# The down product of an MLP on taller tiles: 128 rows by 64 columns in a kernel of 64 by 64 tiles

## The chip, the cores and the metric

The kernel runs on one core of one Trainium2 chip, as a single program. The metric is the device time of one execution in microseconds; the number given for a kernel is the median of its runs. The core has a matrix engine (TensorE, PE in the profile, with its weight loads as PEld), a vector engine (VectorE, DVE), an activation engine (ScalarE, ACT), GpSimd (POOL), and the queue of SyncE (SP), which issues all DMAs of this kernel. Matmuls write into PSUM, which has banks of 512 float32 values in each of 128 partitions.

## The reference

An RWKV-7 recurrence over 768 steps, for 4 sequences and 8 heads of 40 channels, is followed by an MLP with the quick GELU. Everything is float32.

```python
# r, k, v, w, a, b: (4, 8, 768, 40); w_in: (320, 2048); w_out: (2048, 320)
for t in range(S):
    y[:, :, t] = einsum('bhd,bhde->bhe', r_t, state)
    Sa = einsum('bhde,bhe->bhd', state, a_t)
    state = state * w_t[:, :, None, :] - einsum('bhd,bhe->bhde', Sa, b_t) \
            + einsum('bhd,bhe->bhde', v_t, k_t)
x = y.transpose(0, 2, 1, 3).reshape(3072, 320)
h = x @ w_in
g = h * (1.0 / (1.0 + exp(-1.702 * h)))
return g @ w_out                      # (3072, 320)
```

The last line is what the change is about: 3072 tokens, a contraction over 2048, 320 columns out.

## The kernel before

**Units.** The recurrence is done in chunks of 64 steps. A unit is one chunk of two sequences, so there are 24 units (`NU`), two for each of the 12 chunks. For every unit the kernel builds decay factors (`decay`), scaled operands and score matrices (`prep`, PSUM tiles `ps_A` and `ps_RV`), inverts a triangular matrix by repeated products (`inverse`, `ps_N`, five steps `ps_level`, `ps_Q`, `ps_T`), and solves and advances the state (`solve`: `ps_zT`, `ps_rz`, `ps_B`, `ps_X`, `ps_y`). The result goes through DRAM (`x_dram`) and comes back turned as `xT_all`.

**The MLP.** As soon as both units of a chunk are there, `mlp(c)` works on its 256 tokens. `up` computes 128 hidden channels for 256 tokens at a time, `gelu` (L1023) writes them to `g` as float32 with the channels on the partitions: a tile of `g` holds two channel groups `m` of 2 x 128 channels. `down(p)`, for `p` in 0 and 1, contracts them with `w_out_sb`, whose rows are the same channels, into 128 tokens by 320 columns. Its eight parts `part(m)`, for `m` in 0 to 7 (`NM`), each take two groups `f` of 128 channels, and all add into the same pair of PSUM banks.

**Tiles of the array.** Every matmul in the kernel works on a tile of at most 64 rows by 64 columns, and works are laid out in fours, in the order of `QUARTERS`: the row half `r` of the operands and the column half `b` of the output. In the down product the two row halves of a group of 128 channels are contracted in different quarters and land in different banks, `po[HALF[b], r]`. So bank 0 holds the sum over the channels in partitions 0 to 63 and bank 1 that over partitions 64 to 127, and L1047 copies the first to `ob` (on ACT or DVE, whichever is free by the plan) while L1049 adds the second (on DVE). Then `store` (L1046) issues two DMAs to `out`. A float32 product is two MATMUL instructions and two LDWEIGHTS; all are recorded at line 332, the helper `mm`, so the profile is read by tiles: `ps_down` is the down product, `ps_up` the up product. 12 chunks x 2 halves x 8 parts x 2 groups x 4 quarters x 2 instructions are the 3072 matmuls of `ps_down`.

**The order.** Nothing is issued as it is written. Each piece of work is handed to `plan.add` with a rank, a time on each engine that may do it, what it reads and writes, and the PSUM pair that it uses; there are four pairs of banks. `Plan.order` is a simulation in the host program: each engine that comes free takes the task of the lowest rank that is ready. Attention tasks have low ranks and MLP tasks 10000 and up, so the MLP fills the time in which no attention task is ready. PE's tasks also carry `instr`, a number of instructions: the plan believes that PE's instructions are fetched in blocks of 256 (`fetched`, `ahead`), and passes over a task whose instructions would come too late. `paced` spreads the MLP over the time, and `refined` tries 300 random changes to the ranks of the opening's tasks and keeps those that shorten the plan. The order that results is fixed: the engines then run it with semaphores.

The price of a PE task comes from one line:

```python
return {"PE": sum(n * 2 * max(m[0] / 1.2 + 5 if m else 58.0, cols / 1.2 + 3) for n, cols, *m in sets),
        "instr": sum(16 * n for n, *_ in sets)}
```

Of the kernel before, what the change touches and what calls it, by code (L numbers as in the profile page):

```python
# [279 lines left out]
def rwkv7_gelu_quick(ctx: ExitStack, tc: tile.TileContext, time_d, v_d, w_d, wc_d, ak_d, b_d, rv_d, w_in, w_out, out):  # L280
    nc = tc.nc
    H, D, S = 8, 40, out.shape[0] // 4
    DM = H * D
# [7 lines left out]
    NQ = NM // 2  # L291
# [9 lines left out]
    HALF = [slice(0, 64), slice(64, 128)]  # L301
    CHANNELS = [slice(h.start, h.start + D) for h in HALF]
    BITS = (0, 1)
    QUARTERS = [(0, 0), (1, 1), (0, 1), (1, 0)]
# [7 lines left out]
    plan = Plan(dict(logw=3, wc=3, G=1, wch=3, wz=2, time=2, ak=2, b=2, rv=2, FT=3, GT=1, kh=2, bh=2, zr=2, rz=2,  # L312
                     A=1, B=1, RV=2, E0=2, W0=2, P21=2, PT=2, W=2, E=2, ES=2, EX=2, T=2, Tc=1, QT=1, zraw=2, zT=1, M=2, x=1, xT=3, g=4, ob=1), 4)
# [5 lines left out]
    def buf(name, n, shape, dt=FP32):  # L319

        if (name, n) not in tiles:
            s = n % plan.slots[name]
            tiles[name, n] = work.tile(shape, dt, tag=f"{name}{s}", name=name)
        return tiles[name, n]

    def psum(t, name):
        if t.pair not in psums:
            psums[t.pair] = banks.tile([128, 2, 512], FP32, tag=f"pair{t.bank}", name=name)
        return psums[t.pair]

    def mm(o, lhsT, rhs, start):
        nc.tensor.matmul(o, lhsT, rhs, start=start, stop=True, skip_group_check=True)  # L332
# [5 lines left out]
    def pe(*sets):  # L338

        return {"PE": sum(n * 2 * max(m[0] / 1.2 + 5 if m else 58.0, cols / 1.2 + 3) for n, cols, *m in sets), "instr": sum(16 * n for n, *_ in sets)}  # L340

    def dve(n):
        return {"DVE": 170.0 + 1.03 * n}
# [4 lines left out]
    def any2(n):  # L348
        return {**act(n), **dve(n)}

    def copy(e):
        return nc.scalar.copy if e == "ACT" else nc.vector.tensor_copy
# [99 lines left out]
    w_out_sb = w_sb[:, NK * NM * 128:]  # L452
# [555 lines left out]
    ob_of = lambda n: buf("ob", n, [128, DM])  # L1008

    def mlp(c):  # L1010
        R = 10000 + 100 * c

        def up(q, m, k):
            def go(t):
                ph, x = psum(t, "ps_up"), xT_of(c)[:, :, k]
                for r, h in QUARTERS:
                    mm(ph[HALF[h], r, m * 256:(m + 1) * 256], w_in_sb[HALF[r], 2 * q + m, k, h * 64:(h + 1) * 64], x[HALF[r]],
                       m == 0 and k == 0)
            plan.add(R + q, pe((1, 256)), go, reads=[("xs", (c, p)) for p in BITS] + [("weight", q)],
                     uses=[("xT", c)], room=[("g", c * NQ + q)], pair=("up", c * NQ + q), most=1)  # L1020

        def gelu(q):
            plan.add(-45, {"ACT": 1030.0, "table": "gelu"}, lambda t: nc.scalar.activation(  # L1023
                g_of(c * NQ + q).rearrange("p m r n -> p r m n"), psum(t, "").rearrange("p r (m n) -> p r m n", m=2),
                ACT.Gelu_apprx_sigmoid), writes=[("g", c * NQ + q)], pair=("up", c * NQ + q))

        def down(p):
            serial = 2 * c + p

            def part(m):  # L1030
                def go(t):
                    po, g = psum(t, "ps_down"), g_of(c * NQ + m // 2)[:, m % 2]
                    for f in (2 * m, 2 * m + 1):
                        for r, b in QUARTERS:
                            o = p * 128 + b * 64
                            mm(po[HALF[b], r, :DM], g[HALF[r], f % 2, o:o + 64], w_out_sb[HALF[r], f * DM:(f + 1) * DM], f == 0)
                parts = range(2 * m * DM // PIECE, (2 * (m + 1) * DM - 1) // PIECE + 1)
                plan.add(R + 10 * (p + 1) + m, pe((2, 320)), go, reads=[("g", c * NQ + m // 2)] + [("weight", NQ + n) for n in parts],
                         pair=("down", serial), most=1)
            for m in range(NM):  # L1040
                part(m)

            def store(t):
                for b in BITS:
                    o = (2 * p + b) * S + c * C
                    nc.sync.dma_start(out[o:o + C, :], ob_of(serial)[HALF[b]])  # L1046
            plan.add(-45, any2(320), lambda t: copy(t.engine)(ob_of(serial), psum(t, "")[:, 0, :DM]),  # L1047
                     writes=[("ob", serial)], pair=("down", serial))
            plan.add(-45, dve(320), lambda t: nc.vector.tensor_add(ob_of(serial), ob_of(serial), psum(t, "")[:, 1, :DM]),  # L1049
                     reads=[("ob", serial)], writes=[("out", serial)], pair=("down", serial))  # L1050
            plan.add(-100, {"SP": 700.0}, store, reads=[("ob", serial), ("out", serial)], size=128 * DM * 4)

        for q in range(NQ):
            for m in BITS:
                for k in range(NK):
                    up(q, m, k)
            gelu(q)
        for p in BITS:
            down(p)
# [110 lines left out]
```

## Time and profile before

| | |
|---|---|
| median of 3 runs | 695.43 us |
| the runs | 690.06, 695.43, 698.79 us |
| span of the profiled execution | 691.5 us, 42207 instructions |
| its own time | not given apart from the span; the median of the runs stands 3.9 us above the span |
| busy: PE / weight loads / DVE / ACT / POOL | 655.2 / 532.6 / 437.5 / 363.7 / 204.4 us |
| `ps_up` matmuls | 3840, 251.1 us busy, mean 377 ns |
| `ps_down` matmuls | 3072, 238.8 us busy, mean 430 ns |
| `ps_down` weight loads | 3072, 124.8 us busy, mean 133 ns |
| the adds of L1049 | 24, 11.6 us busy, mean 483 ns |
| mean granted TensorE clock | 0.987 |

The busy time of a group is the time in which at least one of its instructions runs, so matmuls that run side by side count once; the mean is that of one instruction. The page cuts the span in 40 slices and gives each engine's busy share in tenths. The chain that ended last follows the work back from the last instruction, at each step to what released it. A number in brackets behind an instruction in a timeline is the engine's idle time before it, and who ended it.

### The profile page before, as it was taken

The page shows a single profiled execution, that of the slowest core. Times are in us where ns is not written, and L with a number is a line of the kernel's source. Part 1 is how long each engine was busy: PE and PEld are TensorE (multiplying, and loading weights), DVE is VectorE, ACT ScalarE, POOL GpSimd, SP SyncE. Part 2 cuts the span into 40 slices and gives each one's busy share as a digit, 9 for nine tenths or more (in the row PEclk, how much of TensorE's full clock was granted, in tenths as well). Part 3 has the DMA queues.
Part 4 walks back from the last instruction along what each step waited for, and adds up shares of the span by engine and source line. Part 5 has one row for each costly group of instructions (what it writes and reads, how often), then busy time and mean ns, then how long its engine had stood idle before and what let it go on. Part 6 is the DMA issues. An engine that isn't in the chain of part 4 may idle for free.

```text
span 691.5 us, 42207 instructions
## 1 busy us (share of the span) xinstructions
PE 655.2 (95%) x19488; PEld 532.6 (77%) x19488; DVE 437.5 (63%) x799; ACT 363.7 (53%) x760; POOL 204.4 (30%) x258
## 2 busy tenths in 40 slices
PE   5676899999999999999999999999999999999997
PEld 4575777878899889878798787787779777786663
DVE  7777888657767667857676856776776656542000
ACT  4566565565555664564645566547555544432020
POOL 6546563232133242343132424222222331100000
PEclk9979999999999999999999999999999999999999
DMA  7985443233322531441331432331431320111000
GB/s 257 344 276 178 143 151 97 80 104 87 98 79 70 135 121 33 120 126 54 110 103 58 124 100 82 109 100 48 136 116 43 108 68 17 42 42 32 21 3 20
DMA packets 35312, 69.73 MB, mean 101 GB/s; under 512 B 5440, under 2 KB 14656, under 8 KB 35136
## 3 DMA queue, kind: packets, MB, share of 16 engines
q1 hardware_dynamic: 35136, 67.03, 32.0%
q8 instruction: 153, 2.51, 1.5%
q14 instruction: 23, 0.19, 0.1%
HBM read 59.15 MB, written 7.86 MB: 97 GB/s over the span
## 4 chain that ended last, share of the span: by engine, by line
PE 88%; DMA 4%; DVE 3%; issue 2%; ACT 2%; SPq 0%; ACTq 0%; DVEq 0%
PE ps_up L332 29%; PE ps_down L332 28%; PE ps_level L332 8%; PE ps_y L332 5%; PE ps_B L332 5%; PE ps_X L332 3%; PE ps_N L332 2%; PE ps_rz L332 1%; DMA time<-in_time 1%; PE ps_RV L332 1%; PE ps_A L332 1%; PE ps_zT L332 1%; DMA w_sb<-in_w_in 1%; PE ps_Q L332 1%; PE ps_cum L332 1%
## 5 line engine op out<-in xcount | busy, mean ns | idle before, releaser
L332 PE MATMUL ps_up<-xT_all,w_sb 64*64 64x256 f32 x3840 | 251.1, 377 | 0.8 <-DVE E L788 0.5
L332 PE MATMUL ps_down<-w_sb,g 64*64 64x320 f32 x3072 | 238.8, 430 | 1.2 <-DVE ob L1049 1.1
L332 PEld LDWEIGHTS ps_up<-xT_all,w_sb 64*64 64x64 f32 x3840 | 153.0, 133 | 30.1 <-issue 1.7
L332 PEld LDWEIGHTS ps_down<-w_sb,g 64*64 64x64 f32 x3072 | 124.8, 133 | 49.9 <-PE ps_RV L332 0.7
L1023 ACT ACTIVATE g<-ps_up 128x1024 f32<-128x1024 f32 x48 | 49.2, 1025 | 34.1 <-PE ps_up L332 33.4
L662 POOL TENSOR_TENSOR kh<-time,G 128x320 f32<-128x320 f32 x24 | 21.8, 906 | 143.2 <-PE ps_y L332 56.9
L332 PEld LDWEIGHTS ps_level<-W,EX 64*64 64x64 f32 x2560 | 56.9, 134 | 8.4 <-issue 0.9
L786 ACT COPY W<-ps_level 128x512 f32<-128x512 f32 x49 | 28.7, 586 | 65.4 <-PE ps_level L332 65.3
L742 ACT ACTIVATE EX<-ES,quads 128x256 f32<-128x256 f32 x92 | 41.7, 501 | 39.1 <-DVE ES L737 39.1
L332 PE MATMUL ps_level<-W,EX 64*64 64x64 f32 (+1 forms) x2560 | 55.5, 218 | 0.0
L788 DVE TENSOR_TENSOR E<-two,ps_level 128x256 f32<-128x256 f32 x80 | 33.2, 415 | 26.3 <-ACT W L786 25.6
L1049 DVE TENSOR_TENSOR ob<-ob,ps_down 128x320 f32<-128x320 f32 x24 | 11.6, 483 | 59.4 <-ACT ob L1047 59.1
L332 PE MATMUL ps_level<-PT,EX 64*64 64x64 f32 (+2 forms) x1280 | 33.9, 238 | 10.7 <-DVE EX L758 5.9
L332 PEld LDWEIGHTS ps_level<-PT,EX 64*64 64x64 f32 x1280 | 31.2, 141 | 16.0 <-issue 4.3
L654 POOL TENSOR_TENSOR ak<-ak,FT 128x512 f32<-128x512 f32 x20 | 27.9, 1394 | 50.8 <-DMA ak<-in_ak 22.7
L926 ACT COPY B<-ps_B 128x416 f32<-128x416 f32 (+1 forms) x39 | 19.1, 491 | 43.2 <-PE ps_B L332 43.2
L737 DVE STREAM_TRANSPOSE ES<-E 128x256 f32<-128x256 f32 x80 | 35.6, 445 | 4.2
L988 POOL TENSOR_TENSOR x<-zr,FT 128x128 f32<-128x128 f32 x72 | 36.1, 530 | 1.8 <-DVE zr L978 1.8
L832 ACT COPY Tc<-ps_level 32x64 f32<-32x64 f32 x134 | 27.1, 202 | 18.1 <-PE ps_level L332 15.9
L732 POOL TENSOR_TENSOR PT<-two,PT 128x256 f32<-128x256 f32 x20 | 14.6, 730 | 72.4 <-DVE PT L724 72.4
L332 PE MATMUL ps_y<-M,bh 64*64 64x104 f32 (+1 forms) x768 | 34.6, 246 | 0.1
L332 PE MATMUL ps_y<-RV,kh 64*64 64x104 f32 (+1 forms) x768 | 34.4, 247 | 0.0
(134 smaller groups left out, 1157.2 us busy)
## 6 DMA issues: line engine op xcount, KB each, us to landing
time<-in_time SPq DMA_DIRECT2D x24, 320.0 KB
ak<-in_ak SPq DMA_DIRECT2D x48, 160.0 KB
rv<-in_rv SPq DMA_DIRECT2D x48, 160.0 KB
xT_all<-x_dram SPq DMA_DIRECT2D x48, 160.0 KB
wc<-in_wc SPq DMA_DIRECT2D x20, 264.0 KB
logw<-in_w SPq DMA_DIRECT2D x24, 160.0 KB
RV<-in_v SPq DMA_DIRECT2D x24, 160.0 KB
b<-in_b SPq DMA_DIRECT2D x48, 80.0 KB
```

What stands on the lines that cost most here:

```text
L332: nc.tensor.matmul(o, lhsT, rhs, start=start, stop=True, skip_group_check=True)
L654: plan.add(R, {"DVE": 690.0, "POOL": 1270.0, "sbuf": True}, lambda t: of(t.engine).tensor_mul(ahT(), ahT(), FT_of(i)), reads=T("ak", "FT") ...
L662: plan.add(R + 4, {"POOL": 870.0, "DVE": 490.0, "sbuf": True}, lambda t, n=n, dst=dst: of(t.engine).tensor_mul(dst(i)[:, :, :D], by_head(t ...
L732: plan.add(R, {"DVE": 430.0, "POOL": 750.0, "sbuf": True}, lambda t: of(t.engine).tensor_sub(at(W0_t, i)[:, :, :32], two32.unsqueeze(1).to ...
L737: plan.add(rank, dve(256), lambda t: nc.vector.transpose(ES(n), source(t)), writes=[key("ES", n, 6)], **reads)
L742: nc.scalar.activation(dst[:, :, h], ES(n), ACT.Copy, scale=quads[:, h, :1])
L786: plan.add(rank, any2(512), lambda t: copy(t.engine)(tiles_of(W(n + 1)), blocks(psum(t, ""), 64)), writes=[key("W", n + 1, 5)], pair=pair)
L788: plan.add(rank, dve(256), lambda t: nc.vector.tensor_sub(tiles_of(E(n + 1)), every(two32, [128, 2, 4, 32]), blocks(psum(t, ""), 64)[:, :, ...
L832: copy(t.engine)(dst, src[:, u, :, f])
L926: plan.add(R, any2(4 * wide), lambda t: copy(t.engine)(dst(), some(psum(t, "")[:, :, :208])), writes=[("Bv", i)] if x and c > 0 else T("B" ...
L988: of(t.engine).tensor_mul(x[:, b ^ u, b], both(i)[:, at, :64], FT_of(i)[:, at])
L1023: plan.add(-45, {"ACT": 1030.0, "table": "gelu"}, lambda t: nc.scalar.activation(g_of(c * NQ + q).rearrange("p m r n -> p r m n"), psum(t, ...
```

## The change

The quarters of the down product become halves: for each group of 128 channels there are two matmuls, one for each column half `b`, with all 128 partitions of `g` as weights (64 tokens, the columns of the tile) and all 128 partitions of `w_out_sb` as the moving operand. Both write to bank 0 of the pair, to partitions 0 to 63 and 64 to 127. The sum over the row halves is made in the contraction, so the second bank stays unused, L1049 goes, and the store waits for the copy of L1047 alone. The plan keeps the old price of a part on PE, and its number of instructions is set from 32 to 16. All other products keep tiles of 64 by 64.

```diff
                     for f in (2 * m, 2 * m + 1):
-                        for r, b in QUARTERS:
+                        for b in BITS:
                             o = p * 128 + b * 64
-                            mm(po[HALF[b], r, :DM], g[HALF[r], f % 2, o:o + 64], w_out_sb[HALF[r], f * DM:(f + 1) * DM], f == 0)
+                            mm(po[HALF[b], 0, :DM], g[:, f % 2, o:o + 64], w_out_sb[:, f * DM:(f + 1) * DM], f == 0)
                 parts = range(2 * m * DM // PIECE, (2 * (m + 1) * DM - 1) // PIECE + 1)
-                plan.add(R + 10 * (p + 1) + m, pe((2, 320)), go, ...
+                plan.add(R + 10 * (p + 1) + m, {**pe((2, 320)), "instr": 16}, go, ...
...
             plan.add(-45, any2(320), lambda t: copy(t.engine)(ob_of(serial), psum(t, "")[:, 0, :DM]),
                      writes=[("ob", serial)], pair=("down", serial))
-            plan.add(-45, dve(320), lambda t: nc.vector.tensor_add(ob_of(serial), ob_of(serial), psum(t, "")[:, 1, :DM]),
-                     reads=[("ob", serial)], writes=[("out", serial)], pair=("down", serial))
-            plan.add(-100, {"SP": 700.0}, store, reads=[("ob", serial), ("out", serial)], size=128 * DM * 4)
+            plan.add(-100, {"SP": 700.0}, store, reads=[("ob", serial)], size=128 * DM * 4)
```

More of the change, by code (lines that the diff above doesn't have):

```diff
@@ L1033, in go @@
                     for f in (2 * m, 2 * m + 1):
-                        for r, b in QUARTERS:
+                        for b in BITS:
                             o = p * 128 + b * 64
-                            mm(po[HALF[b], r, :DM], g[HALF[r], f % 2, o:o + 64], w_out_sb[HALF[r], f * DM:(f + 1) * DM], f == 0)
+                            mm(po[HALF[b], 0, :DM], g[:, f % 2, o:o + 64], w_out_sb[:, f * DM:(f + 1) * DM], f == 0)
                 parts = range(2 * m * DM // PIECE, (2 * (m + 1) * DM - 1) // PIECE + 1)
-                plan.add(R + 10 * (p + 1) + m, pe((2, 320)), go, reads=[("g", c * NQ + m // 2)] + [("weight", NQ + n) for n in parts],
+                plan.add(R + 10 * (p + 1) + m, {**pe((2, 320)), "instr": 16}, go, reads=[("g", c * NQ + m // 2)] + [("weight", NQ + n) for n in parts],
                          pair=("down", serial), most=1)
```

## The prediction

> **What bounds the kernel now.** I read the page first: busy shares, the slices, then the chain that ended last.
>
> ```profile
> PE 655.2 (95%) x19488; PEld 532.6 (77%) x19488; DVE 437.5 (63%) x799; ACT 363.7 (53%) x760; POOL 204.4 (30%) x258
> PE   5676899999999999999999999999999999999997
> ...
> PEclk9979999999999999999999999999999999999999
> ...
> PE 88%; DMA 4%; DVE 3%; issue 2%; ACT 2%; SPq 0%; ACTq 0%; DVEq 0%
> PE ps_up L332 29%; PE ps_down L332 28%; PE ps_level L332 8%; PE ps_y L332 5%; PE ps_B L332 5%; PE ps_X L332 3%; PE ps_N L332 2%; PE ps_rz L332 1%; DMA time<-in_time 1%; PE ps_RV L332 1%; PE ps_A L332 1%; PE ps_zT L332 1%; DMA w_sb<-in_w_in 1%; PE ps_Q L332 1%; PE ps_cum L332 1%
> ...
> L332 PE MATMUL ps_down<-w_sb,g 64*64 64x320 f32 x3072 | 238.8, 430 | 1.2 <-DVE ob L1049 1.1
> ```
>
> TensorE sets the end: 88% of the chain, of which the down product 28%, at full granted clock after the opening. A busy PE need not be a full one, so the second view is the chain in order of time, to see how fast the stream runs; first its last stretch of matmuls, then a piece from the middle.
>
> ```profile
> 671.61 15.12 PE ps_down L332 x224
> ```
>
> ```profile
> 333.77 1.08 PE ps_down L332 x16
> 334.85 0.71 PE ps_B L332 x32
> 335.57 1.08 PE ps_down L332 x16
> 336.64 0.71 PE ps_B L332 x32
> 337.36 1.08 PE ps_down L332 x16
> 338.43 0.46 PE ps_level L332 x32
> ```
>
> 224 matmuls are 56 sets of four quarters, so a set takes 15.12/56 = 0.270 us, although one matmul lasts 430 ns: four quarters stream side by side and the next set starts 160 ns before the last is through. All of the product is 3072/4 = 768 sets, 207 us. In the middle piece a part (16 matmuls, 4 sets) takes 1.08 us, the same rate: there is no slack in it. The piece shows too that single parts of the down product are laid between tasks of the attention. Counted over the whole timeline (fragments of one to three instructions at the seams put to their neighbours), the product stands in 140 stretches, most of one part. The last stretch ends the stream, so there are 140 entries and 139 exits: 279 seams.
>
> The third view, PE's timeline, shows what happens at a seam (start, length, then the work).
>
> ```profile
> 337.15 1.29 PE L332 MATMUL ps_down<-w_sb,g 64*64 64x320 f32 x16
> 338.22 0.67 PE L332 MATMUL ps_level<-W,EX 64*64 64x64 f32 x32
> 338.69 1.29 PE L332 MATMUL ps_down<-w_sb,g 64*64 64x320 f32 x16
> ```
>
> The next task starts 337.15 + 1.29 - 338.22 = 0.22 us before the down matmuls are through, and the next down part 0.20 us before the level is. That overlap is what the whole schedule lives on, and the change touches it.
>
> **Part 1: the streaming.** Removed are 1536 matmuls and 1536 weight loads (f: two tiles for four quarters). A set becomes two tiles of 128 rows by 64 columns, each streaming the same 320 columns. The column halves already run side by side now, and the rows of one tile work at once, so a set stays at 0.270 us and the product at 207 us: cost 0. If the two tiles ran one after the other it would cost 768 x 0.270 = 207 us; that is a rival below. The work does not shrink, because half as many instructions use twice the rows each.
>
> **Part 2: the weight loads.** A load is hidden now: in the view of loads one part's 16 loads run in 0.74 us beside matmuls that take 1.31.
>
> ```profile
> 115.30 0.74 PEld L332 LDWEIGHTS ps_down<-w_sb,g 64*64 64x64 f32 x16
> ```
>
> All 16 are done while the four sets still stream, so a quarter is loaded ahead while its own matmul runs. I take the same for the taller tile: 0. Cover gone, a load holds its tile back by what a matmul of a cold start is longer: this tile's matmuls last 429 ns in the median and at most 480, so 51 ns; per set 51 (both tiles at once) to 102 ns (in turn), 768 sets: 39 to 78 us.
>
> ```profile
> L332 PEld LDWEIGHTS ps_down<-w_sb,g x3072: 129/133/140, 89.8 to 686.0; 64*64 64x64 f32 x192
> L332 PE MATMUL ps_down<-w_sb,g x3072: 426/429/480, 90.0 to 686.3; 64*64 64x320 f32 x192
> ```
>
> The Trainium skill speaks against me here: "TensorE: Matmul & The Clock Gate", Part 3, says that a weight load overlaps running matmuls only where the row group differs. Two tiles of 128 rows always share all row groups, so by this rule no load would hide. The row above contradicts it for the quarters; no run here shows it for 128 rows.
>
> **Part 3: the seams.** All matmuls of the kernel now work on tiles of at most 64 by 64; the only other shapes are parts of such a tile (40 rows, 40 columns). After the change each of the 279 seams is a change from a tile that lies over two row halves to one that lies over one, or back. The trace has no such change, so I bound it. From below: at the seam of down and the 40-row read (in the timeline a stretch of two parts starts at 330.92, plus 2 x 1.08 gives 333.08, and the read starts at 333.10) nothing is lost: 0 ns, 0 us in all. From above: no overlap at all and a whole weight load, 0.22 + 0.133 = 0.35 us, 279 times: 98 us. Between them I take a restart in which the old matmuls must be out of the array before the new tile's weights can go in: the 429 - 270 = 159 ns that a matmul stays behind its stream, plus the 51 ns of an uncovered load: 0.21 us, 279 x 0.21 = 59 us. I choose it and not 0 because one contraction over both row halves needs both at once, so a quarter that is not yet through must hold it up, where the 40-row piece lies in a quarter of its own; the nearest row is then a matmul that starts with nothing loaded ahead. Behind each wait everything on PE is queued, and PE is the bound; ACT's gelu (L1023), DVE's masks and the attention's copies wait for PE and slip with it.
>
> The Trainium skill states that changing the tiling mode drains TensorE ("TensorEngine Tiling (Array Packing)", Key Properties); it gives no time. With it the term cannot be 0; without it the bounds above stand.
>
> **Part 4: the second bank and the add.** 24 tensor_add (L1049) of 486 ns go: 11.6 us of DVE, which has 63% load and is not on the chain, hidden behind PE's stream, 0. If that cover were gone they would have cost 11.6. On the path they stand in two places. At the end:
>
> ```profile
> 686.75 0.43 ACT L1047 COPY ob<-ps_down 128x320 f32<-128x320 f32 x1 [8.19 <-PE ps_down L332]
> 687.21 0.49 DVE L1049 TENSOR_TENSOR ob<-ob,ps_down 128x320 f32<-128x320 f32 x1 [8.12 <-ACT ob L1047]
> 687.73 1.11 SPq L1046 DMA_DIRECT2D out<-ob  x2
> ```
>
> The store is issued about 0.5 us sooner: -0.5. And PE with its loads waited 1.1 + 0.5 = 1.6 us on this add before it could reuse the pair of banks; now it waits for the copy, 0.5 us earlier: take half, -0.8. The store's two issues on SP stay as they are; they only lose a wait.
>
> **Part 5: the planner.** It prices a part as before (2 x 2 x (320/1.2 + 3) = 1079 ns, the 1.08 of the chain) but counts 16 instructions for 32, so its rule on PE's instruction fetch bites less and the order will differ. PE's stream shrinks from 38,976 matmuls and loads by 3072 (8%). From 100 us on, the waits put down to "issue" before PE and its loads add up to some 10 us, so the gain lies between 0 and 10; I take 2, since few of these waits stand at the down product (0.7 before its loads).
>
> The other order may move the opening, where PE idles 19 + 8 = 27 us of the first 100; I set 0 with 5 either way, an estimate of a fifth of that.
>
> **Sum.** 691.5 (span) + 59 - 0.5 - 0.8 - 2 = 747. The page gives a span alone for the profiled execution; the median of the runs, 695.4, stands 3.9 above it, which I add: 751, rounded to **750 us**.
>
> **Rivals.**
>
> Not slower: seams are free (0 ns as at the 40-row seam). Then only part 4 and 5 remain: 695.4 - 1.3 - 0 to 10, so 684 to 694, likeliest 691. For it: no seam in the trace costs anything. Against it: no seam in the trace joins tiles of different heights. It decides when a seam costs less than 1.3 + 2 over 279, about 12 ns. Chance 0.18.
>
> Taller loads are not hidden: 750 + 39 to 78 = 789 to 828. For: no 128-row load in the trace. Against: quarters are loaded under their own matmul. Chance 0.10.
>
> The column tiles run one after the other, so the change does not do what its unchanged price in the plan says: 750 + 207 = 957. Against: column halves already overlap in every set of 0.270 us. Chance 0.06.
>
> The forecast's own case, seams between 51 ns (a load alone, 14 us) and 0.30 us (84 us): chance 0.66, range 706 to 776.
>
> **Range and chances.** From 694 to 800: left out are the gaining part of the first rival (0.11), the upper part of the second (0.03) and the third (0.06). Two per cent, about what a measurement of this kernel tells from no change, is 14 us: faster needs below 681.5, which takes the first rival's whole gain and a luckier opening, 0.05; the same takes the rest of the first rival and seams of barely a load, 0.17; slower the rest, 0.78.
>
> **What will show it.** Right: the down product's part still near 1.08 us inside a stretch of several parts, PE's time between two stretches grown by about 0.2 us at each seam, in the timeline no overlap between down and its neighbours, the last long stretch of 224 (then 112) matmuls still near 15.1 us, a lower share of busy PE. Wrong: seams that overlap by 0.2 us as now (first rival), or a last stretch of 20 us or more (second) or 30 (third). Far fewer stretches than 140 would make my count wrong, not the price.

## The result: 5% slower, and the profile after

The changed kernel takes 729.5 us (median of 4 runs, 728.3 to 730.1) against 694.1 us for the kernel before (4 runs, 690.1 to 698.8). The ratio is 1.050, with a 95% interval of 1.045 to 1.055: 35 us more. The profiled execution has a span of 728.4 us and its own time is 730.1.

From the page of the changed kernel, the lines that answer to those of before:

```profile
PE 693.5 (95%) x17952; PEld 485.9 (67%) x17952; DVE 419.8 (58%) x780; ACT 348.9 (48%) x728; POOL 220.6 (30%) x276
PE   5567999999999999999999999999999999999997
...
PE 87%; DMA 7%; DVE 2%; issue 1%; SPq 1%; POOL 1%; ACT 0%; DVEq 0%; POOLq 0%; ACTq 0%
...
L332 PE MATMUL ps_down<-w_sb,g 128*64 128x320 f32 x1536 | 237.2, 441 | 0.0
```

PE has 1536 matmuls fewer and 38 us more of busy time, and its share is the same 95%. So PE's share does not show where the time went: a matmul's end is modelled, and PE counts as busy through the pauses shown below. The share of the weight loads fell from 77% to 67%, but half as many loads for the down product lower it by themselves: a kernel below that has their old number again is as slow and has 81%. What gives the time away is why the loads were idle. Their row in the page before, then after:

```profile
L332 PEld LDWEIGHTS ps_down<-w_sb,g 64*64 64x64 f32 x3072 | 124.8, 133 | 49.9 <-PE ps_RV L332 0.7
L332 PEld LDWEIGHTS ps_down<-w_sb,g 128*64 128x64 f32 x1536 | 97.9, 136 | 81.6 <-issue 10.8
```

"issue" is time in which an engine waited for nothing that the profile shows. Over all weight loads the waits put to it add up to 19 us before and 68 us after.

The chain in order of time (start, length up to the next piece, work) tells more. First the last stretch of the down product, then a piece from the middle.

```profile
708.87 15.25 PE ps_down L332 x112
```

```profile
344.46 1.23 PE ps_down L332 x8
345.69 1.59 PE ps_B L332 x64
347.28 1.23 PE ps_down L332 x8
348.50 0.62 PE ps_A L332 x32
```

112 matmuls are 56 sets of two tiles in 15.25 us, 0.272 us per set: the taller tile streams at the old rate, side by side, with its loads hidden. But a part between two attention tasks takes 1.23 us instead of 1.08, and the task before a part is longer as well: 64 matmuls of `ps_B` take 1.59, where two pieces of 32 took 0.71 each. So each seam costs some 0.15 to 0.17 us here. The product stands in 138 stretches, so there are 275 seams.

PE's timeline at such a seam (start, length as modelled, work):

```profile
343.85 0.62 PE L332 MATMUL ps_level<-W,EX 64*64 64x32 f32 x32
344.39 1.30 PE L332 MATMUL ps_down<-w_sb,g 128*64 128x320 f32 x8
345.62 0.59 PE L332 MATMUL ps_B<-RV,A 64*64 64x104 f32 x16
```

Of the overlap of 0.22 and 0.20 us before, 343.85 + 0.62 - 344.39 = 0.08 and 0.07 are left. And the tile's view gives the longest matmul, 484 - 432 = 52 ns above the median. Exactly the first two matmuls of each of the 138 stretches are this long: their weights were not loaded ahead.

```profile
L332 PE MATMUL ps_down<-w_sb,g x1536: 432/432/484, 96.0 to 723.7; 128*64 128x320 f32 x192
```

The end of the program, as foreseen, is shorter without the add: from the start of the last copy to the store it is 0.45 us instead of 0.98.

```profile
724.19 0.43 ACT L1047 COPY ob<-ps_down 128x320 f32<-128x320 f32 x1 [8.19 <-PE ps_down L332]
724.64 1.11 SPq L1046 DMA_DIRECT2D out<-ob  x2
```

### The profile page after: what moved, and what is told of

Read it like the earlier page. It is cut to its first block, busy times and chain, and to the rows that moved or that the text cites. A ratio compares the mean times of both kernels' runs of the same rounds, so it can differ in the third digit from the quotient of the medians.

```text
span 728.4 us, 39081 instructions
## 1 busy us (share of the span) xinstructions
PE 693.5 (95%) x17952; PEld 485.9 (67%) x17952; DVE 419.8 (58%) x780; ACT 348.9 (48%) x728; POOL 220.6 (30%) x276
## 4 chain that ended last, share of the span: by engine, by line
PE 87%; DMA 7%; DVE 2%; issue 1%; SPq 1%; POOL 1%; ACT 0%; DVEq 0%; POOLq 0%; ACTq 0%
PE ps_down L332 31%; PE ps_up L332 28%; PE ps_level L332 7%; PE ps_y L332 4%; PE ps_B L332 4%; PE ps_X L332 2%; DMA rv<-in_rv 2%; PE ps_N L332 1%; PE ps_rz L332 1%; PE ps_A L332 1%; PE ps_RV L332 1%; DMA wc<-in_wc 1%; PE ps_zT L332 1%; PE ps_T L332 1%; DMA x_dram<-x 1%
## 5 line engine op out<-in xcount | busy, mean ns | idle before, releaser
L332 PE MATMUL ps_up<-xT_all,w_sb 64*64 64x256 f32 x3840 | 245.5, 379 | 1.1 <-issue 0.5
L332 PE MATMUL ps_down<-w_sb,g 128*64 128x320 f32 x1536 | 237.2, 441 | 0.0
L332 PEld LDWEIGHTS ps_up<-xT_all,w_sb 64*64 64x64 f32 x3840 | 140.5, 134 | 44.7 <-issue 7.7
L332 PEld LDWEIGHTS ps_down<-w_sb,g 128*64 128x64 f32 x1536 | 97.9, 136 | 81.6 <-issue 10.8
L786 ACT COPY W<-ps_level 128x512 f32<-128x512 f32 x57 | 33.4, 586 | 72.6 <-PE ps_level L332 72.5
L742 ACT ACTIVATE EX<-ES,quads 128x256 f32<-128x256 f32 x98 | 44.5, 501 | 37.3 <-DVE ES L737 36.8
L332 PEld LDWEIGHTS ps_level<-W,EX 64*64 64x64 f32 x2560 | 50.2, 134 | 17.8 <-issue 9.5
L988 POOL TENSOR_TENSOR x<-zr,FT 128x128 f32<-128x128 f32 x80 | 41.1, 543 | 3.2 <-issue 2.7
L744 POOL TENSOR_TENSOR EX<-ES,quads 128x512 f32<-128x512 f32 x15 | 20.3, 1351 | 49.4 <-DVE ES L737 47.2
L744 POOL TENSOR_TENSOR T<-ES,quads 128x512 f32<-128x512 f32 x12 | 15.9, 1323 | 58.2 <-DVE ES L737 58.2
```

The costliest lines, as they stand in the source:

```text
L742: nc.scalar.activation(dst[:, :, h], ES(n), ACT.Copy, scale=quads[:, h, :1])
L744: of(t.engine).tensor_mul(dst, ES(n).unsqueeze(2).to_broadcast([128, 8, 2, 32]), quads.unsqueeze(1).to_broadcast([128, 8, 2, 32]))
L786: plan.add(rank, any2(512), lambda t: copy(t.engine)(tiles_of(W(n + 1)), blocks(psum(t, ""), 64)), writes=[key("W", n + 1, 5)], pair=pair)
L988: of(t.engine).tensor_mul(x[:, b ^ u, b], both(i)[:, at, :64], FT_of(i)[:, at])
```

## The experiments

Theory S says that each seam between tile shapes costs about 0.155 us. The rivals are O, that the other order and the other instruction count cost the time, and P, that each set of the taller tile costs more wherever it stands.

**Tile and order apart.** The first kernel has the new tiles in the old order, the second the old tiles in the new order. The second leaves out the sum of the second bank, so its output is not the whole product.

```diff
 e1: the kernel before, with
-  for r, b in QUARTERS: mm(po[HALF[b], r, :DM], g[HALF[r], ...], w_out_sb[HALF[r], ...])
+  for b in BITS:        mm(po[HALF[b], 0, :DM], g[:, ...], w_out_sb[:, ...])
-  lambda t: nc.vector.tensor_add(ob_of(serial), ...)
+  lambda t: None
 e2: the changed kernel, with
-  for b in BITS:        mm(po[HALF[b], 0, :DM], g[:, ...], w_out_sb[:, ...])
+  for r, b in QUARTERS: mm(po[HALF[b], r, :DM], g[HALF[r], ...], w_out_sb[HALF[r], ...])
```

> Taller tiles, but in the order of the kernel before: the plan gets the old number of instructions and the old task of the add, which issues nothing. 140 stretches of the down product, so 279 seams. Theory S (each seam between tiles of 64 by 64 and of 128 by 64 costs about 0.155 us, from the changed kernel's trace: a part takes 1.23 us up to the next task instead of 1.08, and the task before a part 0.16 us longer): 694 + 279 x 0.155 = 737 us, less 1 for the add at the end. Rival O (the other order and instruction count cost the time, the tiles nothing): 694 us. Rival P (each set of the taller tile costs 35/768 = 0.046 us more, seams nothing): 729 us with parts of 1.26 us also inside the last long stretch.

> The changed kernel's order and plan, but the down product in quarters of 64 by 64 again; the sum of the second bank is left out (there is no add). 138 stretches, no seam between shapes. Theory S: 729.5 - 275 x 0.155 = 687 us. Rival O: 729 us. Rival P: 694 us.

The first took 728.9 us, ratio 1.048 (1.042 to 1.053); the second 697.9 us, ratio 1.002 (0.999 to 1.006). The order is worth nothing that can be told from zero, the tiles 31 to 34 us, in either order. O is out. S misses by the same amount in both: it expected some 43 us between the kernels of one order, and the medians differ by 34 and 32 (the spans, 723.3 and 691.5, 728.4 and 697.2, by 32 and 31). In the second kernel's chain a part between two attention tasks takes the old time, so what lengthens it is the shape and not the neighbour:

```profile
345.64 1.08 PE ps_down L332 x16
346.71 0.71 PE ps_B L332 x32
```

The last stretch of the first kernel runs at the old rate too, which speaks against P:

```profile
703.75 15.25 PE ps_down L332 x112
```

**The price of a seam by itself.** Behind the kernel before stands a stage that only changes shapes. It was executed once, so its times are compared with one another, within one trace.

```diff
+    for name, works, n in (("p_q", [(quarters, 320)], 24), ("p_t", [(tall, 320)], 24), ("p_b", [(broad, 320)], 24), ("p_w", [(whole, 320)], 24),
+                           ("p_qt", [(quarters, 320), (tall, 320)], 20), ("p_qt64", [(quarters, 64), (tall, 320)], 20),
+                           ("p_qt4", [(quarters, 320)] * 4 + [(tall, 320)] * 4, 5),
+                           ("p_qb", ...), ("p_qw", ...), ("p_tw", ...), ("p_bw", ...)):
+        for _ in range(n):
+            for work_on, cols in works: work_on(po, cols)
```

> The kernel before with a stage of matmuls behind it that goes to no output: sets of 320 columns in quarters (p_q), tall 128 by 64 (p_t), broad 64 by 128 (p_b), whole 128 by 128 (p_w), then changes from set to set. Theory S: the four plain stretches at 0.27 us per set; p_qt (40 sets, 39 seams) 10.8 + 39 x 0.155 = 16.8 us; p_qt4 (40 sets in fours, 9 seams) 12.2 us; p_qt64 (sets of 64 columns in the quarters) the same price per seam; p_qb, p_qw, p_tw, p_bw also near 16.8 us if any change of tile shape empties the array, and 10.8 us where only the height counts and it stays (p_bw and p_qt change it, p_qb and p_tw do not). Rival (seams cost nothing in themselves): all 10.8 us.

The expectation counted a call as one set; a float32 call is two, so the plain stretches have 48 sets, 13.0 us, and those of 40 calls a base of 80 x 0.270 = 21.6 us. PE's timeline of the stage, in the order of the diff after the first stretch (the three `p_qt` lines are `p_qt`, `p_qt64`, `p_qt4`):

```profile
707.41 13.14 PE L332 MATMUL p_t<-w_sb 128*64 128x320 f32 x96 [0.35 <-DVE ob L1117]
720.88 13.19 PE L332 MATMUL p_b<-w_sb 64*128 64x320 f32 x96 [0.33 <-DVE ob L1117]
734.40 13.19 PE L332 MATMUL p_w<-w_sb 128*128 128x320 f32 x48 [0.33 <-DVE ob L1117]
747.90 27.84 PE L332 MATMUL p_qt<-w_sb 64*64 64x320 f32 x240 [0.32 <-DVE ob L1117]
776.06 19.35 PE L332 MATMUL p_qt<-w_sb 64*64 64x64 f32 x240 [0.33 <-DVE ob L1117]
795.74 23.16 PE L332 MATMUL p_qt<-w_sb 64*64 64x320 f32 x240 [0.33 <-DVE ob L1117]
819.23 28.84 PE L332 MATMUL p_qb<-w_sb 64*64 64x320 f32 x240 [0.33 <-DVE ob L1117]
848.39 28.77 PE L332 MATMUL p_qw<-w_sb 64*64 64x320 f32 x200 [0.33 <-DVE ob L1117]
877.48 28.57 PE L332 MATMUL p_tw<-w_sb 128*64 128x320 f32 x120 [0.32 <-DVE ob L1117]
906.37 29.57 PE L332 MATMUL p_bw<-w_sb 64*128 64x320 f32 x120 [0.32 <-DVE ob L1117]
```

A shape alone, whichever, streams a set in 0.270 us (13.14 less a tail of 0.16, by 48). With a change at each call: (27.84 - 0.16 - 21.6)/39 = 0.156 us per seam. With short sets of 64 columns in the quarters (0.058 us each, as in the kernel's `ps_level`, 32 matmuls or 8 sets in 0.46 us) the base is 40 x 0.270 + 40 x 0.058 = 13.1, and the seam (19.35 - 0.16 - 13.1)/39 = 0.156. With one seam in four calls (23.16 - 0.16 - 21.6)/9 = 0.156. So it is a price per seam, not per set or matmul, and P is out. It is not the change of PSUM bank or of height either: quarters with broad tiles, where both have 64 rows and write to both banks, cost (28.84 - 0.16 - 21.6)/39 = 0.182. Tiles of 128 columns come out dearer: 0.180 (`p_qw`), 0.175 (`p_tw`), and 0.200 where both sides have 128 columns (`p_bw`).

**A full tile in the kernel.** The down product of the changed kernel in 128 by 128, same order.

```diff
-  for b in BITS: mm(po[HALF[b], 0, :DM], g[:, f % 2, o:o + 64], ...)
+  mm(po[:, 0, :DM], g[:, f % 2, p * 128:p * 128 + 128], ...)
```

> The changed kernel's order with the down product in one tile of 128 by 128 (one matmul for the two column halves), the same 138 stretches and 275 seams. Theory S with the price split as the trace shows it (the first set of a stretch takes 0.32 instead of 0.27 us, so 0.05 is the uncovered load of 64 columns and 0.105 the emptying of the array): entries have a load of 128 columns, 0.05 more; 729.5 + 138 x 0.05 = 736 us. Rival (the price is of the load alone, twice as long): 729.5 + 138 x 0.155 = 751 us. If a full tile's loads did not hide, 768 sets x 0.1 us more, 800 us.

It took 737.9 us, ratio 1.057 (1.053 to 1.061), 0.6% above the ratio of the changed kernel: 4 us more by the ratios, 8 by the medians and 6 by the spans (734.2 and 728.4), where 7 were expected; 751 us, for a price that is all load, is out. Its longest matmul tells how the price is made up (this line is of its tile's view):

```profile
L332 PE MATMUL ps_down<-w_sb,g x768: 432/433/538, 96.1 to 729.4; 128*128 128x320 f32 x192
```

A load of 128 columns that is not covered costs 538 - 433 = 105 ns, one of 64 columns 52. So a seam is a pause of 0.156 - 0.052 = 0.104 us, and then the load of the tile that is entered. That the load waits can be seen in the stage, where the weight loads stop before each change (this one is into quarters) and start again only with their own matmuls:

```profile
760.39 0.21 PEld L332 LDWEIGHTS p_qt<-w_sb 64*64 64x64 f32 x8 [0.49 <-issue]
```

That the pause is the array emptying is a reading: the traces show its length, not what happens in it. The two terms are nearly enough for the other pairs. They give 0.104 + (0.052 + 0.105)/2 = 0.182 for a stretch that changes between 64 and 128 columns (measured 0.175 to 0.182) and 0.209 for `p_bw` (0.200).

**More seams with fewer tall sets.** Half of the down product back in quarters, but with a seam inside every part.

```diff
+  if f % 2 == 0:
+      for b in BITS: mm(po[HALF[b], 0, :DM], g[:, ...], w_out_sb[:, ...])
+  else:
       for r, b in QUARTERS: mm(po[HALF[b], r, :DM], g[HALF[r], ...], w_out_sb[HALF[r], ...])
```

> The kernel before, old order and add kept, where each part of the down product does its first group of 128 channels in tall tiles and its second in quarters. Half the tall sets, but every part has an entry and an exit of its own: 2 x 192 = 384 seams for 279. Theory S: 694 + 384 x 0.156 - 9 (what was taken up before) = 745 us. Rival P (each tall set costs 0.046 us): 694 + 384 x 0.046 = 712 us.

746.1 us, ratio 1.071 (1.064 to 1.079): S had 745, P 712. The last stretch of its chain holds 14 parts and so about 28 seams:

```profile
719.83 19.48 PE ps_down L332 x168
```

19.48 - 56 x 0.270 = 4.4 us, 0.156 per seam.

**Where the missing 9 to 10 us went.** In the first experiment 279 seams at 0.156 are 43.5 us, and the time rose by 33 to 34. Theory A says that the seams took up waits of PE that stood there anyway; its rival F, that half the instructions relieve PE's supply of them. The next kernel, in the old order like the first experiment, gives PE its old number of instructions back.

```diff
+  for h in BITS:
       for b in BITS: mm(po[HALF[b], 0, n], g[:, ...], w_out_sb[:, f * DM + n.start:f * DM + n.stop], ...)   # n: 160 columns
```

> The taller tiles in the old order (as the first experiment, 728.9 us, 279 seams) with each matmul cut in two of 160 columns, so that PE's stream has as many matmuls and loads as before the change. The seams should have cost 279 x 0.156 = 43 us there, but the time rose by 34 only; where did 9 us go? Theory A (waits of PE that stood in the old kernel anyway are taken up in the seams): only the shorter matmuls cost, 768 sets x 3 ns = 2 us, so 731 us. Rival F (half the instructions relieve PE's instruction supply, which the split gives back): 731 + 9 = 740 us.

732.9 us, ratio 1.053 (1.046 to 1.060): 4 us above the unsplit kernel by the medians. The 731 of theory A lies in the interval; F's 740 (1.064) lies outside, so F is out. The traces fit A. Taking from each start-to-start time on PE what the matmul's columns need at the streaming rate, the kernel before has 52 us in which PE does not stream, 39 of them in the first 100 us. Of the other 13, 4.6 stand where a down part meets its neighbours. In the first experiment, in the same order, the seams hold 41.3 us and all else 43.0, where it was 47.2. So by this count the gross price is 41 us, 4.6 of it lies on waits that stood there anyway, and 4.2 more are won elsewhere: 41.3 - 4.6 - 4.2 - 0.5 (the end) = 32.0, and the spans differ by 31.8. Where a seam is taken to begin and end moves some 2 us between the seams and the rest; the sum stays. That less is lost elsewhere because whoever PE waited for has more time is the likely reason; no run shows it by itself.

**Fewer seams.** More parts of the down product in one task of the plan: two, four or all eight; and the control, the kernel before with two or four.

```diff
-  for f in (2 * m, 2 * m + 1):
+  for f in range(2 * m, 2 * m + 2 * G):        # G = 2, 4, 8
```

> The changed kernel with two parts of the down product in one task of the plan: 81 stretches, 161 seams, the same matmuls. Theory S: 114 seams less, 729.5 - 114 x 0.155 = 712 us, if longer tasks in PE's queue cost the attention nothing. Rivals O and P: 729 us (P has the same 768 sets; O an order that differs again but no price for seams).

> The changed kernel with four parts of the down product in one task of the plan: 44 stretches, 87 seams. Theory S: 729.5 - 188 x 0.155 = 700 us, and more than that by what tasks of 4.4 us on PE cost the attention that waits behind them. Rivals O and P: 729 us or more.

> The changed kernel with all eight parts of the down product in one task: 22 stretches, 43 seams. Theory S: 729.5 - 232 x 0.155 = 694 us if the attention paid nothing for tasks of 8.6 us on PE; I expect it to pay, so 700 to 715 us. Rivals O and P: 729 us or more.

> The control for two parts in a task: the kernel before (quarters, add kept) with 80 stretches and no seam between shapes. The tall kernel with two parts in a task took 727.4 us where 712 was expected. If longer tasks ate the 16 us, this one takes some 10 to 15 us more than the kernel before, 704 to 709 us; if it takes 694, long tasks are free and the price of a seam was not what fell away.

> A control: the kernel before (quarters, add kept) with four parts of the down product in one task: 44 stretches, no seam between shapes. It prices long tasks alone. If they cost nothing, 694 us; if the attention pays for them, more, and the same amount has to be taken off the taller kernel with four parts.

| parts in a task | tall: us, ratio | seams | quarters: us, ratio |
|---|---|---|---|
| 1 | 729.5, 1.050 (1.045 to 1.055) | 275 | 694.1, 1 |
| 2 | 727.4, 1.047 (1.041 to 1.053) | 161 | 707.3, 1.016 (1.010 to 1.022) |
| 4 | 751.0, 1.081 (1.074 to 1.089) | 87 | 732.9, 1.046 (1.041 to 1.052) |
| 8 | 762.0, 1.090 (1.086 to 1.095) | 43 | not run |

The expectations missed: the seams fell away, and the time did not. The controls say why. Long tasks on PE cost the kernel 1.6% and 4.6% with no seam at all. By the count above, PE does not stream for 13 us after the first 100 in the kernel before, and for 21 and 47 us in the two controls. The likely reason is that the attention, whose chain of small tasks has to go on, waits behind the long ones; no run separates this from the changed order. With two parts the tall kernel stands 0.030 above its control, some 21 us, for 161 seams (25 gross). With four it stands 0.035 above by the ratios, 24 us, but 18 by the medians and 16 by the spans (747.6 and 731.9), where 87 seams make 14 us gross. The ratios rest here on runs of two chips, and the orders of these two kernels differ, as the plan sees other instruction counts, so whether more than the seams lies between them stays open. No version of these beats the kernel before.

## Why the prediction was right, by its own steps

The forecast was slower, 750 us, in a range of 694 to 800; measured was 729.5.

- **The streaming** was put at 0: right, 0.272 us per set in the kernel and 0.270 in the stage by itself. Two tall tiles run side by side.
- **The weight loads** of tall tiles were put at 0, as hidden: right by the same rows. The rule of the Trainium skill ("TensorE: Matmul & The Clock Gate", Part 3), that loads overlap only matmuls of another row group, would have them uncovered in every set; 48 sets of `p_t` in 13.1 us and of `p_w` in 13.2 leave no room for a load of 0.052 or 0.105 us per set.
- **The seams** were the term that decided, right in kind and in number (279 foreseen, 275 found), and too dear: 0.21 us against 0.156. The load was right (51 against 52 ns). What failed is the step that took a matmul's modelled length less its stream, 159 ns, for the time in which the array empties. That pause is 104 ns: the next tile starts while the modelled ends of the last matmuls still have 0.07 to 0.08 us to run. The lower bound that came from the 40-row seam did not apply: beside tiles of 64 by 64 a piece of 40 rows cost nothing, and a tile of 128 rows did. The rule of the Trainium skill ("TensorEngine Tiling (Array Packing)", Key Properties), that a change of the tiling mode drains TensorE, agrees with every change tried here, at 0.156 to 0.200 us.
- **The add** and the end: -0.5 us foreseen, -0.53 found. PE's waits for the add before a part are gone (idle before `ps_down` 0.0 for 1.2).
- **The planner**: the new order is worth 0.2% (interval -0.1 to 0.6%) by the second experiment; 0 with 5 either way was put for it. The 2 us of relief of PE's instruction supply were not found.
- **What the sum lacked**: a price on the engine that sets the end was added whole. Some 9 to 10 of the 43 us fell on waits that stood there or were won back elsewhere. Of the 20 us between forecast and result the size of the seam makes 15 (279 x 0.054). These 9 to 10 are more than the rest, and against them stand the relief of 2 us that did not come and some 2 us for the order, within its noise.

Two of the signs that were named did not come: some overlap is left at a seam, and PE's busy share did not fall (95% both times). The growth at each seam, 0.15 to 0.17 us for the 0.2 foreseen, and the unchanged last stretch did. In the first rival, 695.4 - 1.3 - 2 is 692, not 691; nothing rests on it.

## What to carry to other kernels

A change of the PE tile shape has a price that PE's busy time does not show: here a pause of 0.10 us and then the uncovered load of what comes next, for every change tried between four shapes in float32, in rows or columns. A shape that is better by itself (half the instructions, no add behind it) must be weighed against the number of times that the schedule lays it beside another, and where small tasks are woven together, one shape for all of them is worth an extra add. Clearing the seams away by longer tasks is no free remedy either: price it with a control that has the long tasks and no seams.

## What the runs showed of the hardware that was not expected

The price of a seam hardly depends on what changes: 64 by 64 beside 64 by 128 costs as much (0.182 us) as beside 128 by 128 (0.180), and the other pairs differ mostly by the load. It is also the same after a set of 64 columns as after one of 320 (0.156 both). And the profile books this time as work: PE's busy share was 95% with and without 275 seams, and only the start-to-start times in the chain and the idle time of the weight loads that is put to "issue" gave it away: 19 us before, 24 in the quarters of the new order, and 51 to 68 in the three kernels with all parts in tall tiles, one part to a task. The busy share of the loads is no such sign, with 77% before, 67% after, and 81% in the equally slow kernel whose matmuls are cut in two.
